# Score matmuls in bursts of three row-tiled pairs, with a hand-made order for the rest

The kernel runs on one core of a Trainium2 chip. The metric is the device time of one execution in microseconds (us). A run is called fast when it lies within 1.5% of the fastest of its kernel.

## The reference, cut to what matters

For each of 8 batches, with S = 3200 positions, D = 256 and a score width of 64:

```python
scores = (1.0 / S) * (z @ z.T)                 # z: S x 64, so S x S scores
x = u * (np.maximum(scores, 0.0) ** 2 @ v)     # u, v: S x 256
wq, wk = x @ w_q, x @ w_k                      # S x 64
mixed = (1.0 / 8.0) * (wq @ wk.T) @ x          # linear, so it can be x @ J with a 256 x 256 J
out = np.maximum(mixed, 0.0) @ w_out
```

Both kernels use `mixed = x @ (w_q w_k' (x'x)) / 8`. They need the sum x'x over all rows (X'X below), then a small matrix J, then two products per group of rows: `mx` (with J, then relu) and `fo` (with w_out). The large work is the scores and the product with v: 25 x 25 tiles of 128 x 128 per batch. In these kernels the operands of TensorE lie in a memory called SBUF, and its results in one called PSUM, which the kernels divide into banks. "Gate" below is relu and scaling of a score tile in PSUM, followed by a square into fp16 in SBUF.

## The kernel before

Score tiles are made in pairs. The 64 columns of z lie in SBUF twice, on partitions 0-63 and again on 64-127. One matmul of a pair uses the upper half of the array's rows and the other the lower half ("row tiling"), so that the two can run at once. A pair's out matmuls (with v) follow three pairs later. Which instruction comes when is left to the framework's scheduler, with priorities.

```python
psc = ... bufs=4, PSUM    # score tiles, one bank each
pacc = ... bufs=1, PSUM   # accumulator of a group of 512 or 384 columns, two banks
ptp = ... bufs=2, PSUM    # transposes, X'X, mx, fo
...
for pair in tpairs:                                  # two tiles, the last one alone
    for ti in pair:
        sc_ps = psc.tile([P, SG], FP32, tag="sc", name="sc_ps")
        half = (ti % 2) * dqk
        nc.tensor.matmul(out=sc_ps[:, 0:gw],
                         lhsT=zT2[half : half + dqk, ts(ti, P)],
                         rhs=zT2[half : half + dqk, ds(gs, gw)], start=True, stop=True)
    ...                                              # gate on VectorE (16 of 20) or ScalarE,
    ...                                              # square on ScalarE or GpSimd
    pending.append((ats, gi, out_ps, u_sb))
    if len(pending) > DEPTH:                         # DEPTH = 3
        emit_outs(*pending.pop(0))
# emit_outs: for each tile, gw // 128 matmuls of 256 columns into out_ps;
# at a group's end x = out_ps * u on VectorE, then transposes of x on TensorE
...
# emit_XJ(b), after a batch: 50 matmuls for X'X, then copy, product, copy, product, copy -> J
# emit_MX_chunk(b, jt, gi): mx and fo of the batch before, at the start of each group
```

Of the kernel before, what the change touches and what calls it, by code (L numbers as in the profile page):

```python
# [12 lines left out]
SQUARE = mybir.ActivationFunctionType.Square  # L13
# [4 lines left out]
def kernel(  # L18
# [10 lines left out]
    nc = tc.nc  # L29
# [6 lines left out]
    SG = 512  # L36
    sgroups = []
    s0 = 0
    for w in [512, 512, 512, 512, 384, 384, 384]:
        sgroups.append((s0, w))  # L40
        s0 += w
    assert s0 == S
    ND = D // P
    XPRI = 4 << 20
    SUPRI = 3 << 20
    HIPRI = 2 << 20
    MIPRI = 1 << 20
    DEPTH = 3
    tpairs = []
    ti = 0  # L50
    while ti < NT:
        tpairs.append(tuple(range(ti, min(ti + 2, NT))))
        ti += 2

    GSCALE = 4.0
    C1 = GSCALE * GSCALE
    ALPHA = C1 * float(S) * float(S)
    FINAL_SCALE = 1.0 / (8.0 * ALPHA * ALPHA * ALPHA)

# [5 lines left out]
    pg = ctx.enter_context(tc.tile_pool(name="pg", bufs=10))  # L65
    pat = ctx.enter_context(tc.tile_pool(name="pat", bufs=12))
    pjt = ctx.enter_context(tc.tile_pool(name="pjt", bufs=2))
    prt = ctx.enter_context(tc.tile_pool(name="prt", bufs=3))
    pfo = ctx.enter_context(tc.tile_pool(name="pfo", bufs=4))
    pmisc = ctx.enter_context(tc.tile_pool(name="pmisc", bufs=2))  # L70
    psc = ctx.enter_context(tc.tile_pool(name="psc", bufs=4, space=bass.MemoryType.PSUM))
    pacc = ctx.enter_context(tc.tile_pool(name="pacc", bufs=1, space=bass.MemoryType.PSUM))
    ptp = ctx.enter_context(tc.tile_pool(name="ptp", bufs=2, space=bass.MemoryType.PSUM))

    def emit_consts():
      ident32 = consts.tile([P, P], FP32, tag="ident32")
      make_identity(nc, ident32)
      ident = consts.tile([P, P], FP16, tag="ident")
      make_identity(nc, ident)

      wqk32 = consts.tile([P, 2, 2 * dh], FP32, tag="wqk32")
      nc.sync.dma_start(out=wqk32[:, :, 0:dh], in_=moe_w_q.rearrange("(c p) h -> p c h", p=P))
      nc.sync.dma_start(out=wqk32[:, :, dh : 2 * dh], in_=moe_w_k.rearrange("(c p) h -> p c h", p=P))
      wqT = consts.tile([P, D], FP32, tag="wqT")
      for ac in range(ND):
        wq_tp = ptp.tile([P, P], FP32, tag="tp", name="wq_tp")
        nc.tensor.transpose(wq_tp[0:dh, :], wqk32[:, ac, 0:dh], ident32)
        nc.scalar.copy(out=wqT[0:dh, ts(ac, P)], in_=wq_tp[0:dh, :])

      wo32 = consts.tile([P, 2, D], FP32, tag="wo32")  # L90
      nc.sync.dma_start(out=wo32[:], in_=moe_w_out.rearrange("(c p) e -> p c e", p=P))
      wo = consts.tile([P, 2, D], FP16, tag="wo")
      nc.vector.tensor_copy(out=wo[:], in_=wo32[:])
      return ident32, ident, wqk32, wqT, wo

    st = {}
    ld = {}

    def emit_load(b):
        z32 = pmisc.tile([P, NT, dqk], FP32, tag="z32")  # L100
        nc.sync.dma_start(out=z32[:], in_=z[b].rearrange("(n p) k -> p n k", p=P))
        zs = pmisc.tile([P, NT, dqk], FP16, tag="zs")
        nc.vector.tensor_copy(out=zs[:], in_=z32[:])
        zst = pmisc.tile([P, NT, dqk], FP16, tag="zst")
        nc.vector.transpose(out=zst[:, :, :], in_=zs[:, :, :])  # L105
        zT2 = pzt.tile([P, S], FP16, tag="zT2")
        for bk in range(dqk // 32):
            for bp in range(4):
                nc.sync.dma_start(
                    out=zT2[ds(32 * bk, 32), :].rearrange("j (n bp i) -> j n bp i", bp=4, i=32)[  # L110
                        :, :, bp, :
                    ],
                    in_=zst[ds(32 * bp, 32), :, ds(32 * bk, 32)],
                )
        nc.sync.dma_start(out=zT2[dqk : 2 * dqk, :], in_=zT2[0:dqk, :])
        v_sb = pv.tile([P, NT, D], FP16, tag="v_sb")
        nc.gpsimd.dma_start(out=v_sb[:], in_=v[b].rearrange("(n p) d -> p n d", p=P))
        ld[b] = (zT2, v_sb)

    def emit_A(b, mx_prev=None):  # L120
        zT2, v_sb = ld[b]
        x_sb = px.tile([P, NT, D], FP16, tag="x_sb")
        xT_sb = px.tile([P, ND, S], FP16, tag="xT_sb")
        st[b] = (x_sb, xT_sb)

        u_re = u[b].rearrange("(n p) d -> p n d", p=P)
        nat = 0

        def emit_outs(ats, gi, out_ps, u_sb):
            gs, gw = sgroups[gi]  # L130
            ngb = gw // P
            for ti, at in ats:
                for j in range(ngb):
                    nc.tensor.matmul(  # L134
                        out=out_ps[:, j // 2, ds((j % 2) * D, D)],
                        lhsT=at[:, ts(j, P)],
                        rhs=v_sb[:, ti, :],
                        start=(ti == 0 and j % 2 == 0),
                        stop=(ti == NT - 1 and (j % 2 == 1 or j == ngb - 1)),
                    )  # L140
            if ats[-1][0] == NT - 1:
                xtp = ptp.tile([P, ND, ngb, P], FP16, tag="tp", name="xtp")
                for j in range(ngb):
                    sb = gs // P + j
                    with tc.high_priority(offset=XPRI):
                        nc.vector.tensor_mul(  # L146
                            out=x_sb[:, sb, :],
                            in0=out_ps[:, j // 2, ds((j % 2) * D, D)],
                            in1=u_sb[:, j, :],
                        )  # L150
                    for db in range(ND):
                        nc.tensor.transpose(  # L152
                            xtp[:, db, j, :], x_sb[:, sb, ds(db * P, P)], ident
                        )
                for db in range(ND):
                    with tc.high_priority(offset=HIPRI):
                        nc.scalar.copy(out=xT_sb[:, db, ds(gs, gw)], in_=xtp[:, db])  # L157

        pending = []
        for gi, (gs, gw) in enumerate(sgroups):  # L160
            if mx_prev is not None:
                emit_MX_chunk(*mx_prev, gi)
            ngb = gw // P
            nbank = (ngb + 1) // 2
            out_ps = pacc.tile([P, nbank, 2 * D], FP32, tag="acc", name="out_ps")
            u_sb = pu.tile([P, ngb, D], FP32, tag="u_sb")
            nc.sync.dma_start(out=u_sb[:], in_=u_re[:, gs // P : gs // P + ngb, :])
            for pair in tpairs:
                ats = []
                for ti in pair:  # L170
                    sc_ps = psc.tile([P, SG], FP32, tag="sc", name="sc_ps")
                    half = (ti % 2) * dqk
                    nc.tensor.matmul(  # L173
                        out=sc_ps[:, 0:gw],
                        lhsT=zT2[half : half + dqk, ts(ti, P)],
                        rhs=zT2[half : half + dqk, ds(gs, gw)],
                        start=True,
                        stop=True,
                    )
                    ats.append((ti, sc_ps))  # L180
                for k, (ti, sc_ps) in enumerate(ats):
                    at = pat.tile([P, SG], FP16, tag="at")
                    g32 = pg.tile([P, SG], FP32, tag="g32")
                    m = nat % 20
                    with tc.high_priority(offset=SUPRI):
                        if m < 4:
                            nc.scalar.activation(
                                out=g32[:, 0:gw], in_=sc_ps[:, 0:gw], func=RELU, scale=GSCALE
                            )
                        else:  # L190
                            nc.vector.tensor_scalar(  # L191
                                out=g32[:, 0:gw], in0=sc_ps[:, 0:gw], scalar1=0.0,
                                scalar2=GSCALE, op0=AOP.max, op1=AOP.mult,
                            )
                    eng_act = (k + (nat // 2)) % 2 == 0
                    with tc.high_priority(offset=HIPRI):
                        if eng_act:
                            nc.scalar.square(out=at[:, 0:gw], in_=g32[:, 0:gw])  # L198
                        else:
                            nc.gpsimd.tensor_mul(  # L200
                                out=at[:, 0:gw], in0=g32[:, 0:gw], in1=g32[:, 0:gw]
                            )
                    nat += 1
                    ats[k] = (ti, at, eng_act)
# [137 lines left out]
```

## Time and profile before

The median was 1151.04 us (three runs, 1149.85 to 1153.22).

| | before |
|---|---|
| span of the profiled run | 1147.9 us |
| TensorE busy | 1067.0 us, 93% |
| next busiest, VectorE | 738.0 us, 64% |
| granted TensorE clock, mean | 0.989 |
| runs of score matmuls on TensorE (my count over the trace) | 701 |
| first score matmul | 31.8 us |

The head of the profile's page has, per engine, busy time, its share of the span, and the number of instructions. PE is TensorE, PEld its weight loads, DVE VectorE, ACT ScalarE and POOL GpSimd.

```profile
span 1147.9 us, 21719 instructions
PE 1067.0 (93%) x7890; PEld 637.7 (56%) x7890; DVE 738.0 (64%) x1329; ACT 679.2 (59%) x1355; POOL 665.7 (58%) x712
```

TensorE is the only engine near its limit, but 93% busy does not say that it streams without pause: an out matmul is booked as busy for 276 ns on average, while in a stream the next one starts after 109 ns. The timeline of TensorE in the middle of a 512-column group shows the pattern. Columns: start, length of the merged row (both us), engine, line, operation, tiles and count.

```profile
500.45 0.39 PE L173 MATMUL sc_ps<-zT_4064 64*128 64x512 f16 x2
500.77 1.05 PE L134 MATMUL out_ps<-v_sb,at 128*128 128x256 f16 x8
501.75 0.39 PE L173 MATMUL sc_ps<-zT_4064 64*128 64x512 f16 x2
502.07 1.05 PE L134 MATMUL out_ps<-v_sb,at 128*128 128x256 f16 x8
```

A period is 1.30 us: two score matmuls and eight out matmuls. The single records of the trace show where it goes (start in us, step from the start before in ns):

```
501.433  109   out matmul
501.543  110   out matmul, last of eight
501.748  205   score matmul, rows 0-63
501.751    3   score matmul, rows 64-127
502.070  319   out matmul, first of the next eight
502.189  119   out matmul
```

The two score matmuls do run together, 3 ns apart. But the step into them is 205 ns where out matmuls are 109 ns apart, and the step out is 319 ns where 512 columns in a stream without a change of tiling take 216 ns (seen in mx). Each trip into row tiling and back loses about 0.2 us, once per pair. The list of waits (who waited for what: total us, times, longest) shows the way in as "issue" in front of the weight loads of the scores, line 173, and also shows transposes waiting for x, line 152. These are the three rows with the most time in PE and PEld:

```profile
PEld L173 <- issue: 172.1, 703, 5.6
PEld L134 <- issue: 94.5, 449, 1.1
PEld L152 <- DVE x_sb L146: 53.9, 120, 0.8
```

This list counts idle time of the weight loads, which can stand still while TensorE streams; the single records are the measure of a trip. And not all of the 172.1 us are trips.

The Trainium skill, "TensorEngine Tiling (Array Packing)", Key Properties, says that changing the tiling mode drains TensorE. This trace agrees in that both steps across a change are longer than the ordinary ones, and gives the price.

### The profile page before, as it was taken

To read this page: it belongs to the slowest core of one execution; us is meant where nothing else is said; L and a number is where in the kernel's file an instruction comes from. 1 tells how busy PE (TensorE), PEld (TensorE's weight loads), DVE (VectorE), ACT (ScalarE), POOL (GpSimd) and SP (SyncE) were. 2 spreads that over 40 slices of the span, in tenths; PEclk is the share of its full clock that TensorE was granted. 3 is DMA by queue.
4 is the path that set the end of the run, shared out by engine and by line. 5 is a ranking of instruction groups with operands and counts; after the bars stand their busy time and mean duration, and the time that the engine had idled before them with its cause. 6 is when DMAs were issued, how large, how long until landed. Compare 5 with 4: busy or idle time off the path is not lost. (4 is left out here: it accounts for less than half of the span.)

```text
span 1147.9 us, 21719 instructions
## 1 busy us (share of the span) xinstructions
PE 1067.0 (93%) x7890; PEld 637.7 (56%) x7890; DVE 738.0 (64%) x1329; ACT 679.2 (59%) x1355; POOL 665.7 (58%) x712
## 2 busy tenths in 40 slices
PE   0899989999899998999979999999999999999996
PEld 0356555565555655555545555656565555656563
DVE  1497747677467764676736777477756776567760
ACT  0456646666466664666637665666656667566655
POOL 1468645666456664665636666467655666556650
PEclk9999999999999998999989999999999999999999
DMA  9843172011711128120181212711163112111103
GB/s 179 176 90 72 33 107 73 33 61 49 121 56 51 43 65 123 38 65 29 65 124 38 65 43 57 129 59 33 61 95 98 49 46 65 38 56 47 42 16 114
DMA packets 159132, 80.43 MB, mean 70 GB/s; under 512 B 81457, under 2 KB 158513, under 8 KB 159025
## 3 DMA queue, kind: packets, MB, share of 16 engines
q1 hardware_dynamic: 133296, 65.95, 22.7%
q0 software_dynamic: 25728, 13.11, 8.6%
q8 instruction: 61, 1.00, 0.4%
q14 instruction: 47, 0.38, 0.1%
HBM read 59.38 MB, written 26.21 MB: 75 GB/s over the span
## 5 line engine op out<-in xcount | busy, mean ns | idle before, releaser
L134 PE MATMUL out_ps<-v_sb,at 128*128 128x256 f16 x5000 | 670.8, 276 | 1.4 <-ACT at L198 1.4
L134 PEld LDWEIGHTS <-at 128*128 128x128 f16 x5000 | 443.2, 98 | 167.5 <-issue 94.5
L157 ACT COPY xT_sb<-xtp 128x512 f16<-128x512 f16 (+1 forms) x112 | 55.0, 543 | 44.0 <-PE xtp L152 43.6
L146 DVE TENSOR_TENSOR x_sb<-out_ps,u_sb 128x256 f16<-128x256 f32 x200 | 70.9, 414 | 14.3 <-PE out_ps L134 14.3
L273 ACT ACTIVATE rt<-mx_ps 128x512 f16<-128x512 f32 (+1 forms) x112 | 58.9, 555 | 28.2 <-PE mx_ps L265 28.1
L280 PE MATMUL fo_ps<-wo,rt 128*128 128x256 f16 x400 | 66.1, 286 | 8.1 <-ACT rt L273 5.2
L173 PE MATMUL sc_ps<-zT_103 64*128 64x512 f16 (+1 forms) x175 | 40.8, 380 | 34.0 <-DMA zT_103<-zst 31.8
L289 ACT ACTIVATE fo_sb<-fo_ps 128x512 f32<-128x512 f32 x112 | 56.0, 551 | 19.9 <-PE fo_ps L280 16.8
L265 PE MATMUL mx_ps<-xT_sb,jt 128*128 128x512 f16 (+1 forms) x224 | 60.3, 357 | 2.4 <-ACT rt L273 1.7
L152 PEld LDWEIGHTS <-x_sb 128*128 128x128 f16 x400 | 26.3, 97 | 63.4 <-DVE x_sb L146 53.9
L280 PEld LDWEIGHTS <-rt 128*128 128x128 f16 x400 | 34.4, 101 | 40.1 <-ACT rt L273 31.4
L152 PE MATMUL xtp<-ident,x_sb 128*128 128x128 f16 x400 | 53.3, 223 | 2.8 <-DVE x_sb L146 0.5
L105 DVE STREAM_TRANSPOSE zst<-zs 128x1600 f16<-128x1600 f16 x8 | 14.7, 1840 | 50.1 <-DMA u_sb<-in_u_dram 14.0
L220 PE MATMUL xtx_ps<-x_sb 128*128 128x256 f16 x400 | 46.8, 273 | 0.0
L173 PE MATMUL sc_ps<-zT_6108 64*128 64x512 f16 (+1 forms) x175 | 36.9, 365 | 6.6 <-DVE g_8223 L191 5.6
L173 PE MATMUL sc_ps<-zT_121 64*128 64x512 f16 (+1 forms) x175 | 36.6, 363 | 5.1 <-DVE g_2091 L191 3.9
L173 PE MATMUL sc_ps<-zT_4064 64*128 64x512 f16 (+1 forms) x175 | 37.1, 367 | 4.6 <-DVE g_6179 L191 3.6
L173 PE MATMUL sc_ps<-zT_2020 64*128 64x512 f16 (+1 forms) x175 | 37.1, 367 | 4.5 <-DVE g_4135 L191 3.5
L220 PEld LDWEIGHTS <-x_sb 128*128 128x128 f16 x400 | 38.1, 98 | 4.0
L173 PEld LDWEIGHTS <-zT_103 64*128 64x128 f16 x175 | 9.5, 93 | 54.4 <-DMA zT_103<-zst 31.8
L173 PE MATMUL sc_ps<-zT_12240 64*128 64x512 f16 (+1 forms) x175 | 36.1, 362 | 1.0 <-DVE g_14615 L191 0.2
L173 PE MATMUL sc_ps<-zT_10196 64*128 64x512 f16 (+1 forms) x175 | 36.1, 362 | 1.0 <-DVE g_12882 L191 0.2
(2838 smaller groups left out, 2120.4 us busy)
## 6 DMA issues: line engine op xcount, KB each, us to landing
out_dram<-fo_sb SPq DMA_DIRECT2D x88, 256.0 KB, 2.2
u_sb<-in_u_dram SPq DMA_DIRECT2D x32, 512.0 KB, 3.9
v_sb<-in_v_dram POOLq DMA_DIRECT2D x8, 1600.0 KB, 16.4
u_sb<-in_u_dram SPq DMA_DIRECT2D x24, 384.0 KB, 3.2
out_dram<-fo_sb SPq DMA_DIRECT2D x24, 128.0 KB, 2.1
z_97<-in_z_dram SPq DMA_DIRECT2D x1, 800.0 KB, 5.5
z_115<-in_z_dram SPq DMA_DIRECT2D x1, 800.0 KB, 21.2
z_2014<-in_z_dram SPq DMA_DIRECT2D x1, 800.0 KB, 9.8
```

The source lines that it names most:

```text
L105: nc.vector.transpose(out=zst[:, :, :], in_=zs[:, :, :])
L134: nc.tensor.matmul(out=out_ps[:, j // 2, ds((j % 2) * D, D)], lhsT=at[:, ts(j, P)], rhs=v_sb[:, ti, :], start=(ti == 0 and j % 2 == 0), st ...
L146: nc.vector.tensor_mul(out=x_sb[:, sb, :], in0=out_ps[:, j // 2, ds((j % 2) * D, D)], in1=u_sb[:, j, :],)
L152: nc.tensor.transpose(xtp[:, db, j, :], x_sb[:, sb, ds(db * P, P)], ident)
L157: nc.scalar.copy(out=xT_sb[:, db, ds(gs, gw)], in_=xtp[:, db])
L173: nc.tensor.matmul(out=sc_ps[:, 0:gw], lhsT=zT2[half : half + dqk, ts(ti, P)], rhs=zT2[half : half + dqk, ds(gs, gw)], start=True, stop=True,)
L220: nc.tensor.matmul(out=xtx_ps[:, cc, :], lhsT=x_sb[:, ti, ds(cc * P, P)], rhs=x_sb[:, ti, :], start=(ti == 0 and cc == 0), stop=(ti == NT ...
L265: nc.tensor.matmul(out=mx_ps[:, 0:gw], lhsT=jt[:, ac, ds(db * P, P)], rhs=xT_sb[:, ac, ds(gs, gw)], start=(ac == 0), stop=(ac == ND - 1),)
L273: nc.scalar.activation(out=rt[:, db, 0:gw], in_=mx_ps[:, 0:gw], func=RELU)
L280: nc.tensor.matmul(out=fo_ps[:, j - jf, :], lhsT=rt[:, dc, ts(j, P)], rhs=wo[:, dc, :], start=(dc == 0 and j == jf), stop=(dc == ND - 1 an ...
L289: nc.scalar.mul(out=fo_sb[:, 0:nj, :], in_=fo_ps[:, 0:nj, :], mul=FINAL_SCALE)
```

## The change

The intent is to pay the trip less often. The scores of six tiles (three pairs, in six PSUM banks) are made in one burst; then come the out matmuls of the burst before, with one piece of the other work ("filler": transposes with X'X, or J, or one mx, or one fo) in their middle. The order is written by hand. Gates and squares become 1024 columns wide. Groups are six of 512 columns and one of 128, in which up to four tiles share one bank. J is made from a precomputed w_q w_k', without two of its copies. The start loads only batch 0. The conversion and transposes of the next batch's z are cut into five pieces, one per burst. The core of the diff, with cuts marked:

```diff
-    for w in [512, 512, 512, 512, 384, 384, 384]:
+    while s0 < S:
+        w = min(BANK, S - s0)            # six of 512, one of 128
...
+    PAIRS = 3
+    BURST = 2 * PAIRS
+    bursts = [list(range(i, min(i + BURST, len(units)))) for i in range(0, len(units), BURST)]
-    psc = ... bufs=4   pacc = ... bufs=1   ptp = ... bufs=2
+    psc = ... bufs=3, PSUM   # slots of two banks: a score pair, or a filler
+    pacc = ... bufs=2, PSUM  # one bank each
...
+    def scores(members):                 # a pair: row half h, bank h of a slot
+        ps = slot("sc_ps")
+        for h, i in enumerate(members):
+            r = ds(h * dqk, dqk)
+            for t, c in pieces:
+                nc.tensor.matmul(out=ps[:, h, ds(c, gw)], lhsT=zT2[r, ts(t, P)],
+                                 rhs=zT2[r, ds(gs, gw)], start=..., stop=...)
...
+    def outs(members, at_middle, ready):  # at_middle: the filler
+        for (b, g), part in segs:         # units of the old group, then of the new one
+            if ends:                      # the group ends in this burst
+                for k in range(nk):
+                    for i in part:
+                        out_mms(i, k)
+                        step(width(i) // P // nk)
+                    x_make(b, g, k)       # VectorE: x = acc * u, frees the bank
...
+        for n, members in enumerate(bursts):
+            for pr in pairs:
+                tiles.append(scores(pr))
+            for q, pr in enumerate(pairs):
+                g32 = gate(tiles[q], pr, "act" if q == 1 else "dve")
+                ...                       # squares: q 0 GpSimd, q 1 ScalarE, q 2 later
+            outs(prev, middle, lambda i: rank[i])
+            for a in late:                # squares of q 2, one GpSimd, one ScalarE
+                square(*a)
```

## The prediction, made without seeing the result

> **What bounds it now.** TensorE. The busy table has PE at 93% of the 1147.9 us span, every other engine at 64% or less; the granted clock is 0.99. But busy is not streaming. Single records in the timeline (500 to 506 us, 512-wide group) show a period of 1.30 us per pair of score tiles: eight out matmuls 109 ns apart, then two score matmuls (rows 0-63 and 64-127) that start 3 ns apart and run together. The step from the last out matmul to the scores is 205 ns, not 109, and from the scores to the next out matmul 320 ns where 512 columns need some 213. So each round trip between full and row-tiled matmuls costs about 0.2 us. The Trainium skill ("TensorEngine Tiling (Array Packing)", Key Properties) says that changing the tiling mode drains TensorE; this trace agrees, and the list of waits books it as "issue" before the score weight loads: 172 us in 703 waits (some of it would be ordinary spacing). I count 701 runs of score matmuls. The rest of the loss: the start (first matmul at 31.8 us, behind the z placement), transposes waiting for x (54 us in 120 waits), XJ's serial chain of four copies per batch, and the tail.
>
> **What the change does.** 210 bursts of three pairs replace 701 runs. Where two pairs already ran back to back (87.0 us) they are 226 ns apart. A burst should cost 205+226+226+310-109, about 0.86 us; three single pairs cost 3x0.42=1.25 us. Saved: 0.39x210, about 80 us. Transposes and X'X move into one filler per burst, J loses two of its copies, the start no longer loads batch 1.
>
> TensorE afterwards, from measured spacings: outs 5000x0.109=544; scores with switches 185; transposes 22; X'X 44; mx 43; fo 44; f32 products for J 16. Sum about 898 us.
>
> Added outside that:
> - start: first burst near 26 us (only v of batch 0 competes with the z placement);
> - tail: seven mx-ACT-fo-ACT links, each about 3.1 us, over what TensorE needs there: 15 us;
> - group ends: x is made on VectorE behind both gates of the burst (two of about 1.15 us), and the next group's accumulator waits for it; by how much of the old group lies in the burst 0 to 2.5 us, mean about 1, x56: 50 us;
> - fillers whose PSUM slot comes back late, SyncE held by z placement, other: 20 us.
>
> That is about 1010 us with the 3 us by which the time exceeds the profile's span.
>
> **Other engines.** From 512- and 384-wide durations: 1024-wide ops need about 1.15 us on VectorE and 0.95 us on ScalarE, a 512-wide square 1.0 us on GpSimd. Per burst (TensorE about 4.3 us): VectorE 2.3 plus x work, ScalarE 2.4 plus 0.95 for a filler, GpSimd 3.0. None is the bound; the margin on ScalarE is the smallest.
>
> **Predicted:** 1010 us, range 960 to 1065. Faster by over 2%: 0.95; within 2%: 0.03; slower: 0.02.
>
> **What would show it right.** About 210 runs of score matmuls; pairs in a burst 226 ns apart; out matmuls still 109 ns apart; "issue" before score loads about 50 us; first matmul near 26 us; PE waits of 0.5 to 2.5 us at group ends, released by the multiplication that makes x; tail after the last out matmul 25 to 30 us.
>
> **What would make it wrong.** Pairs inside a burst not overlapping (weights of the next pair waiting for a drain: 370 ns apart) would cost some 60 us. Six score banks plus a filler share three slots: if evictions come late, every burst waits (0.3 us each is 60 us). If group ends hide, it is nearer 960.

## More of the kernel before

At four of the seven batch changes a score matmul waited 3.5 to 5.6 us, 16.6 us in all, for a gate on VectorE, and VectorE in turn stood 11.8 to 14.0 us in front of a transpose of a later batch's z. The first of the four:

```profile
171.21 1.84 DVE L105 STREAM_TRANSPOSE zst<-zs 128x1600 f16<-128x1600 f16 x1 [12.29 <-DMA zT_2020<-zst]
172.98 0.65 DVE L191 TENSOR_SCALAR g_2091<-sc_ps 128x512 f32<-128x512 f32 x1
173.69 0.37 PE L173 MATMUL sc_ps<-zT_121 64*128 64x512 f16 x1 [3.93 <-DVE g_2091 L191]
```

## The result

The median after was 1019.52 us (four runs, 1017.16 to 1020.08), before 1152.13 us (four runs). The ratio is 0.885, with a 95% interval of 0.883 to 0.887. Ratios here are from fast runs alone, and so not quite the ratio of the medians that are quoted.

The head of the page after, same columns:

```profile
span 1018.2 us, 19437 instructions
PE 922.2 (91%) x7896; PEld 659.3 (65%) x7896; DVE 654.4 (64%) x723; ACT 662.1 (65%) x754; POOL 671.6 (66%) x675
```

TensorE issued the same number of matmuls, within six, and was busy 145 us less; no other engine is near its limit. Its timeline in the first group (line 297 is the scores, 358 the out matmuls):

```profile
31.30 0.82 PE L297 MATMUL sc_ps<-zT_110 64*128 64x512 f16 x6
32.06 2.79 PE L358 MATMUL acc<-v_sb,at 128*128 128x256 f16 x24
34.78 0.82 PE L297 MATMUL sc_ps<-zT_110 64*128 64x512 f16 x6
35.54 0.72 PE L358 MATMUL acc<-v_sb,at 128*128 128x256 f16 x5
```

The period for three pairs is 3.48 us, against 3 x 1.30 = 3.90 us before. In single records, later in the run:

```
504.674  109   out matmul, last before the burst
504.879  205   score matmul      504.883    4   score matmul
505.105  222   score matmul      505.108    3   score matmul
505.321  213   score matmul      505.324    3   score matmul
505.633  309   out matmul
```

The trip is as dear as before (205 in, 309 out), but there are 209 of them instead of 701, and inside the burst pairs follow at the pace of their columns, 226 and 216 ns from the first matmul of a pair to the first of the next. From the list of waits after (other rows left out):

```profile
PEld L358 <- issue: 148.4, 256, 2.3
PE acc L358 <- DVE x_sb L376: 58.7, 69, 2.1
PEld L297 <- issue: 57.0, 212, 10.8
PE sc_ps L297 <- DMA zT_110<-zst: 10.1, 1, 10.1
```

"Issue" in front of the score loads fell from 172.1 (16.6 of it the four waits for a gate) to 57.0 us (10.8 of it once, at the start). The row of the out loads, line 358, grew, but the weight loads also stand still while TensorE itself waits for x or streams a burst, so it is no loss of its own. In place of the trips stands a wait that was not there before: out matmuls of a new group wait for the multiplication that makes x, because it frees the accumulator's bank. The timeline of all engines around the first such wait shows the order that causes it:

```profile
42.25 1.23 DVE L323 TENSOR_SCALAR g_391<-sc_ps 128x1024 f32<-128x1024 f32 x1 [1.12 <-PE sc_ps L297]
42.83 0.27 PE L358 MATMUL acc<-v_sb,at 128*128 128x256 f16 x1
43.39 1.22 DVE L323 TENSOR_SCALAR g_400<-sc_ps 128x1024 f32<-128x1024 f32 x1
44.52 1.28 DVE L376 TENSOR_TENSOR x_sb<-acc,u_sb 128x512 f16<-128x512 f32 x2
45.25 0.38 PE L358 MATMUL acc<-v_sb,at 128*128 128x256 f16 x2 [2.15 <-DVE x_sb L376]
```

TensorE finished the old group near 43.1 us, VectorE made both gates of the burst first, and x began at 44.52 us.

### The profile page after: what moved, and what is told of

Read it like the earlier page. It is cut to its first block, busy times and chain, and to the rows that moved or that the text cites. A ratio compares the mean times of both kernels' runs of the same rounds, so it can differ in the third digit from the quotient of the medians.

```text
span 1018.2 us, 19437 instructions
## 1 busy us (share of the span) xinstructions
PE 922.2 (91%) x7896; PEld 659.3 (65%) x7896; DVE 654.4 (64%) x723; ACT 662.1 (65%) x754; POOL 671.6 (66%) x675
## 5 line engine op out<-in xcount | busy, mean ns | idle before, releaser
L358 PE MATMUL acc<-v_sb,at 128*128 128x256 f16 x5000 | 624.1, 274 | 60.8 <-DVE x_sb L376 58.7
L259 ACT ACTIVATE rt<-mx_ps 128x1024 f16<-128x1024 f32 (+1 forms) x56 | 52.1, 930 | 34.8 <-PE mx_ps L251 34.8
L376 DVE TENSOR_TENSOR x_sb<-acc,u_sb 128x512 f16<-128x512 f32 (+1 forms) x104 | 66.4, 662 | 6.6 <-PE acc L358 5.9
L217 DVE COPY xT_sb<-xx_ps 128x1024 f16<-128x1024 f16 (+1 forms) x56 | 35.5, 634 | 53.2 <-PE xx_ps L210 52.6
L277 ACT ACTIVATE fo_sb<-fo_ps 128x1024 f32<-128x1024 f32 (+1 forms) x56 | 52.1, 930 | 21.3 <-PE fo_ps L269 18.3
L210 PE MATMUL xx_ps<-x_sb 128*128 128x256 f16 x400 | 55.9, 283 | 0.0
L127 POOL DMA_DIRECT2D v_sb<-in_v_dram x40 | 36.4, 910 | 0.8 <-POOLq L513 0.8
L297 PE MATMUL sc_ps<-zT_110 64*128 64x512 f16 (+1 forms) x175 | 23.7, 372 | 13.8 <-DMA zT_110<-zst 10.1
L205 PE MATMUL xx_ps<-ident,x_sb 128*128 128x128 f16 x400 | 32.8, 225 | 0.5 <-DVE x_sb L376 0.5
L225 DVE TENSOR_TENSOR xtx<-xx_ps,xtx 128x512 f32<-128x512 f32 x48 | 32.7, 681 | 0.0
L297 PE MATMUL sc_ps<-zT_773 64*128 64x512 f16 (+1 forms) x175 | 21.7, 356 | 0.0
L297 PE MATMUL sc_ps<-zT_10136 64*128 64x512 f16 (+1 forms) x175 | 21.7, 356 | 0.0
L297 PE MATMUL sc_ps<-zT_3823 64*128 64x512 f16 (+1 forms) x175 | 21.7, 356 | 0.0
L297 PE MATMUL sc_ps<-zT_5390 64*128 64x512 f16 (+1 forms) x175 | 21.7, 356 | 0.0
```

What stands on the lines that cost most here:

```text
L127: nc.gpsimd.dma_start(out=st[b]["v"][:, ds(c * n, n), :], in_=v[b].rearrange("(n p) d -> p n d", p=P)[:, ds(c * n, n), :],)
L205: nc.tensor.transpose(tp[:, db, j, :], x_sb[:, gs // P + j, ds(db * P, P)], cst["ident"])
L210: nc.tensor.matmul(out=ps[:, 1, ds(cc * D, D)], lhsT=x_sb[:, gs // P + j, ds(cc * P, P)], rhs=x_sb[:, gs // P + j, :], start=(j == 0 and c ...
L217: nc.vector.tensor_copy(out=xT_sb[:, :, ds(gs, gw)].rearrange("p d (j s) -> p d j s", s=P), in_=tp[:, :, 0:n, :],)
L225: nc.vector.tensor_add(out=xtx[:], in0=acc, in1=xtx[:])
L259: nc.scalar.activation(out=rt[:, :, 0:gw], in_=ps[:, :, 0:gw], func=RELU)
```

## The experiments

All nine kernels gave a correct result. Medians are of four runs; the kernel before had medians of 1151.2 to 1151.6 us beside them, so they can be compared with 1019.5 us (after) within a microsecond or so.

| run | median us | ratio to before |
|---|---|---|
| after | 1019.52 | 0.885 |
| e1 single pairs | 1105.61 | 0.961 |
| e2 two pairs and one | 1057.63 | 0.919 |
| e3 after without row tiling | 1096.61 | 0.952 |
| e4 narrow gates | 1025.74 | 0.891 |
| e5 before without row tiling | 1122.16 | 0.974 |
| e6 fillers in one lump | 1115.67 | 0.970 |
| e7 x before the second gate | 984.73 | 0.855 |
| e8 filler at the group's end | 1003.59 | 0.872 |
| e9 combination | 962.81 | 0.837 |

**Theory:** the gain is the number of trips between full and row-tiled matmuls. **Rival A:** it is the hand-made order. **Rival B:** it is the wider, fewer evictions. **Rival C:** row tiling pays as such, in both kernels.

### e1 and e2: the same instructions, more trips

The gates and squares move with their pairs, so the order on VectorE, ScalarE and GpSimd changes too, and not on TensorE alone; the numbers of instructions are those of after.

```diff
-            for pr in pairs:
-                tiles.append(scores(pr))
-            ... gates of all three pairs ...
-                outs(prev, middle, lambda i: rank[i])
+            place(first)                 # scores and gates of the first pair (e2: two pairs)
+            outs(prev, middle, ..., [(1 / 3, place(1)), (2 / 3, place(2))])   # e2: [(1 / 2, place(2))]
```

> The kernel after, with its three score pairs of a burst spread over the burst: one pair, a third of the out matmuls, the next pair, and so on. Same instructions on all engines, only their order on TensorE differs; about 628 runs of score matmuls instead of 209. Theory (the round trip between full and row-tiled matmuls is what was saved): a lone pair costs 205+309-109 = 405 ns against 843 ns for three together, so +0.37 us for each of 209 bursts, +78 us: about 1097 us, less perhaps 20 us because the x multiplications now come before the last gate and the group-end waits shrink. Rival (the gain is from the hand-made order, wider evictions and fillers, not from the bursts): within 1% of 1020 us.

> As the single-pairs run, but two pairs together and the third after half of the out matmuls: about 419 runs of score matmuls. Theory: half the dose, +0.18 us for each of 209 bursts, +39 us, about 1058 us, less up to 15 us at group ends. Rival: within 1% of 1020 us.

Measured: 1105.61 us with 625 runs of score matmuls and 1057.63 us with 417, against 1019.52 us with 209. Thus 208 trips more cost 38 us and 416 more cost 86 us: 0.18 and 0.21 us each. In the single records, the steps from matmul to matmul at their usual spacing, without waits, add up to 42 us more in e2 and 84 us more in e1, which is 0.20 us a trip both times. e2 as a whole looks cheaper because its profile has two stretches at half the TensorE clock, where those of after and e1 have six (see e7). The timeline of e1 has the period of the kernel before again, 1.30 us a pair:

```profile
516.69 0.39 PE L298 MATMUL sc_ps<-zT 64*128 64x512 f16 x2
517.01 1.05 PE L359 MATMUL acc<-v_sb,at 128*128 128x256 f16 x8
517.99 0.39 PE L298 MATMUL sc_ps<-zT 64*128 64x512 f16 x2
518.31 1.05 PE L359 MATMUL acc<-v_sb,at 128*128 128x256 f16 x8
```

So 86 of the 132 us that the change gained hang on the bursts; rival A is left with 46 us at most. e1 came out 9 us above the expectation for two reasons that the trace shows. A lone pair costs 205 + 320 - 109 = 416 ns, not the 405 that I had put down with the burst's exit of 309 ns: three lone pairs (1248 ns) against a burst (850 ns) are then 398 ns, times 209 bursts 83 us. And the group-end waits did not shrink (56.7 us of idle time against 58.7):

```profile
PE acc L359 <- DVE x_sb L377: 56.7, 61, 2.0
```

### e3 and e5: no row tiling, in both kernels

All 128 rows are used, that is both copies of z; the score is doubled and the gate's scale halved, so the result is the same.

```diff
-            r = ds(h * dqk, dqk)         # e5: lhsT=zT2[half : half + dqk, ...] likewise
+            r = ds(0, 2 * dqk)           # e5: zT2[:, ...]
-                ... scale=GSCALE / scalar2=GSCALE
+                ... scale=GSCALE / 2 / scalar2=GSCALE / 2
```

> The kernel after without row tiling: each score matmul uses all 128 rows (both copies of z, so twice the score; the gate's scale is halved, the result is the same). No change of mode, but the score matmuls of a pair run one after the other, 216 ns each. Theory: no 205 and 309 ns steps any more, spacing 109 to 216 throughout; scores cost about 272 us instead of 184 us, so +88 us, about 1108 us. If row tiling inside a burst were not what makes scores cheap, the time would stay near 1020 us.

> The kernel before without row tiling (all 128 rows, twice the score, gate scale halved; same result). Theory: a lone row-tiled pair costs 205+320-109 = 416 ns at 512 columns against 432 ns without tiling, 364 against 324 ns at 384 columns, and a lone single tile 416 against 216 ns, so in the kernel before row tiling was worth nothing: about 1125 us, between 1105 and 1150. Rival (row tiling pays in the kernel before as well): 1230 us or more, because 700 pairs would each lose some 0.2 us of overlap.

| | row-tiled | all rows |
|---|---|---|
| order of before | 1151.6 | 1122.2 |
| order of after | 1019.5 | 1096.6 |

This is the clearest result. In the kernel before, taking the row tiling out made it 2.6% faster (ratio 0.974, interval 0.972 to 0.977). In the kernel after, taking it out cost 77 us, where 88 were expected: the steps into, inside and out of the score runs grew by 90 us, but the idle time at group ends fell from 58.7 to 50.9 us. A burst of six then takes 1.30 us from its first matmul to the first out matmul (e3):

```profile
503.32 1.46 PE L297 MATMUL sc_ps<-zT 128*128 128x512 f16 x6
504.62 1.47 PE L358 MATMUL acc<-v_sb,at 128*128 128x256 f16 x12
```

The timeline of e5 shows the kernel before without row tiling:

```profile
501.17 0.59 PE L173 MATMUL sc_ps<-zT 128*128 128x512 f16 x2
501.60 1.04 PE L134 MATMUL out_ps<-v_sb,at 128*128 128x256 f16 x8
502.47 0.59 PE L173 MATMUL sc_ps<-zT 128*128 128x512 f16 x2
```

The score matmuls now run one after the other, 216 ns each, but the steps into and out of them are ordinary. The period is 1.30 us, the same as with row tiling: the overlap of a lone pair (213 ns) and its trip (0.2 us) cancel. By the steps in the trace of before, a 384-column pair cost 205+3+265-109 = 364 ns with row tiling against 2 x 163 = 326 without, and a lone single tile some 416 against 216 ns. The trace of before has 108 lone tiles, 240 lone pairs of 384 columns and 290 of 512 columns, so 108 x 0.20 + 240 x 0.038 - 290 x 0.016 = 26 us is my estimate for these three, near the 29 us measured, though no run takes them apart. The Trainium skill gives "Up to 2×" for a dimension of 64 or less ("TensorEngine Tiling (Array Packing)", Theoretical Speedup); here a lone pair got nothing, and a burst of three took 850 ns where 6 x 216 = 1296 would stand. Rival C falls.

The right column also bounds rival A in another way: without row tiling in either, the new order is worth 26 us, start and batch changes included.

### e4: narrow gates

```diff
     def areas(members):
         ws = [width(i) for i in members]
-        if len(set(ws)) == 1:
-            return [(0, len(ws), ws[0])]
         return [(h, 1, w) for h, w in enumerate(ws)]
```

> The kernel after with every 1024-wide gate and square issued as two 512-wide ones (VectorE and ScalarE instructions rise by about 420 each). Rival theory (the gain comes from fewer and wider evictions): a visible loss, 20 us or more. Theory (TensorE bounds, the other engines have room): the gates take some 0.1 us longer per burst, so only the group-end waits grow, by up to 8 us: 1018 to 1030 us.

Measured 1025.74 us, 6 us more; the steps of TensorE around scores kept their sums. Rival B falls: the halved instruction counts of VectorE and ScalarE, though the most visible difference in the page's head, are worth about half a percent.

### e6: the fillers in one lump

```diff
         if not hit:
             at_middle()
+        if any(f[0] == 1 for f in fillers):    # the batch is complete
+            while fillers:
+                run_filler()
```

> The kernel after, but at the end of a batch all of its fillers (J and the fourteen mx and fo pieces) run one after the other instead of one per burst. Same instructions. Theory (one filler per burst hides ScalarE's links): each batch pays what the tail of the kernel after shows, 25.7 us from the last x to the last eviction against 13 us of TensorE work, so about 12 us more for each of 7 batches: 1090 to 1115 us. Rival (the placing of the fillers is worth nothing): within 1% of 1020 us.

Measured 1115.67 us, 96 us more than after. The list of waits of e6 names the largest part: fo waits for ScalarE's relu of mx, 56 times.

```profile
PE fo_ps L269 <- ACT rt L259: 66.5, 56, 1.2
PE acc L358 <- DVE x_sb L376: 64.8, 79, 2.1
```

In the kernel after the same wait stands at 8.3 us in 7 times, all in the tail, so this wait is 58 of the 96 us. The rest, in J's links, the group ends and slow-clock steps among others, was not taken apart. So one filler per burst is hardly a source of gain over the kernel before, where TensorE's idle time in front of fo was only 8.1 us in all, but bursts without it would have given back more than they won.

### e7 and e8: the wait at group ends

In these two the edits are cut to their sense:

```diff
+            early = any(i in prev[:3] for i in last_of.values())   # e7: group ends early in the burst
             for q, pr in enumerate(pairs):
-                gate and square of q
+                if not (early and q == 2): gate and square of q
 ...
                     x_make(b, g, k)
+                gate and square of q 2, if held back                # e7
+                if not hit and fillers: hit = True; at_middle()     # e8
```

> The kernel after, but in a burst that finishes a group with its first three units or fewer, VectorE makes x before the second gate. TensorE's order is unchanged. Theory (x waits behind the gate): the trace of after shows x starting 1.4, 1.0 and 0.5 us after TensorE began to wait in these bursts; moved up, about 22 us of the 62 us of group-end waits go: about 998 us. Rival (the wait is the multiplication itself and the signalling, not the queue): within 0.5% of 1020 us.

> The kernel after, but a burst that finishes a group before its middle puts its filler right there instead of at the middle. Theory: the filler's 0.9 us of TensorE work covers part of the wait for x in two of six positions of the group end, where one is on hand; about 16 us less: about 1004 us. If the wait is not for x: no change.

e8 came out at 1003.59 us, as expected in the sum but partly by luck: the idle time at the group ends fell by 12.8 us where 16 were expected of it, and the slow steps that the next paragraphs count fell too, from 9.4 to 3.7 us.

```profile
PE acc L358 <- DVE x_sb L376: 45.9, 67, 2.1
```

e7 gave 984.73 us, 35 us less than after, where 22 were expected; the order of TensorE's instructions is exactly that of after. Around the first group end of e7, x now follows the first gate:

```profile
42.67 1.23 DVE L323 TENSOR_SCALAR g<-sc_ps 128x1024 f32<-128x1024 f32 x1 [1.12 <-PE sc_ps L297]
43.81 1.28 DVE L376 TENSOR_TENSOR x_sb<-acc,u_sb 128x512 f16<-128x512 f32 x2
44.55 0.38 PE L358 MATMUL acc<-v_sb,at 128*128 128x256 f16 x2 [1.02 <-DVE x_sb L376]
45.01 1.22 DVE L323 TENSOR_SCALAR g<-sc_ps 128x1024 f32<-128x1024 f32 x1
```

Summed over the trace, the excess of the steps that wait for x over 109 ns fell from 70.0 us in after to 44.4 us in e7. That is 26 us. Another 8 us are slow steps elsewhere: matmuls with nothing to wait for, but more than 20 ns above their usual spacing, add up to 9.4 us in after and 1.4 us in e7. The windows view of after, at one of these stretches, shows the reason (columns: window, length, busy us and count for PE, PEld, DVE, ACT, POOL, then the granted clock, the DMA share and GB/s):

```profile
470.00:478.00 8.00, 6.49 (x56) 4.38 (x55) 6.45 (x7) 5.22 (x6) 5.79 (x7) 1.00 0.01 3
480.50:483.20 2.70, 2.70 (x14) 1.82 (x12) 1.29 (x2) 0.00 (x0) 0.00 (x0) 0.50 0.43 151
```

TensorE had waited 1.71 us for x until 478.20 us, and from 480 us its clock was halved for about 3 us. In after, the six such stretches between the start and the last batch all follow a group-end wait of 1.7 to 2.15 us (some waits of that length had no such sequel). In e7 I find none, and its four runs had a mean granted clock of 0.997 to 0.999 against 0.989 to 0.992 in after.

But the length of a wait does not decide it: after has 16 waits of 1.71 us or more and six halvings, e8 has seven (two of 2.15 us) and none. In the clock records of each profile the changes lie whole multiples of 3.413 us apart. Cut into such stretches, the one before each of the six halvings had TensorE idle for 52 to 69% of it; among the others of after the most is 55%. In e7, e8 and e9, none of which has a halving before its last batch ends, the idlest stretch has 43, 52 and 36%; in e1, 49% was enough. So what seems to count is whether idle time fills about half of one such stretch, and the group-end waits supply much of that idle time. This is argued from the traces, not isolated by a run.

### e9: a version to beat both

It has the edits of e7 and e8. The last batch runs its mx one ahead of its fo, with fo evicted by VectorE. z of the first batch is turned by TensorE transposes instead of by VectorE and small DMAs.

> A version meant to beat both: the kernel after with x before the second gate and the filler at the group end (the two earlier runs together), the last batch's mx pieces one ahead of its fo pieces with fo's eviction on VectorE, and z of the first batch turned by TensorE instead of by VectorE and small DMAs. Theory, from the trace of after: group ends 62 us down to about 25, tail 29 us down to about 21, first score burst from 20.5 to 24.3 us down to about 12: about 962 us, between 945 and 985.

Measured 962.81 us (962.69 to 964.80), ratio 0.837 to before. The sum was right, the parts less so. The first out matmul came at 16.77 us instead of 27.86. The excess at group ends fell to 31.8 us. The tail, from the last out matmul to the end, only fell from 29.3 to 25.9 us, because the evictions now wait for output buffers still being written out:

```profile
947.84 1.23 DVE L313 TENSOR_SCALAR fo_sb<-fo_ps 128x1024 f32<-128x1024 f32 x1 [1.96 <-DMA out_dram<-fo_sb]
950.45 1.22 DVE L313 TENSOR_SCALAR fo_sb<-fo_ps 128x1024 f32<-128x1024 f32 x1 [1.39 <-DMA out_dram<-fo_sb]
```

## Why the prediction was right

It said 1010 us, range 960 to 1065; the result was 1019.52. Point by point:

| step | predicted | measured |
|---|---|---|
| runs of score matmuls | 210 | 209 |
| pair to pair inside a burst | 226 ns | 226 and 216 ns |
| cost of a burst over the outs | 0.86 us | 0.85 us (205+4+222+3+213+3+309-109 = 850 ns) |
| gain from the bursts | 80 us | 86 us (e1) |
| out matmuls apart | 109 ns | 109 ns |
| "issue" before score loads | 50 us | 57.0 us |
| TensorE's own work | 898 us | 894 us |
| start | first burst near 26 us | first scores 20.5 and 24.3 us, first out 27.9 us |
| tail after the last out matmul | 25 to 30 us | 29.3 us |
| waits at group ends | 50 us, 0 to 2.5 each | 70.0 us (58.7 us as idle time), up to 2.15 each |

"TensorE's own work" measured is the sum of the usual spacings of all matmuls outside scores (690.4 us), the steps inside bursts (100.6 us) and those into and out of them (116.4 us), less 14 us that the first two of these waited for z.

The reason it held is that each term was a spacing read from the old trace times a count read from the diff, and the one figure that the old pattern rarely showed, how pairs follow each other without a change of tiling, could be found in a place where two pairs happened to be adjacent (87.0 us). The mechanism that e1, e2, e3 and e5 confirm is the one it named. Its "ScalarE has the smallest margin, none is the bound" also held, with ScalarE at 65%.

The term most off was the group ends, by 20 us: the wait was predicted with its right cause (x behind both gates of the burst, shown by e7), but the mean over the six positions was taken as about 1 us where 70.0 / 56 = 1.25 us was measured. The slow steps after long waits, 9.4 us, were not in the list by name; "other, 20 us" covered them. That the sum missed by less than 10 us is in part luck: the group ends were 20 us too small, "other" and TensorE's own work together some 15 us too large.

The prediction did not divide the 46 us between before and e1: it named the start, the transposes waiting for x, J's chain and the tail as further losses, and not the stops of VectorE at batch changes. The traces place most of them. In the start, the 33rd out matmul came at 48.24 us in before and at 34.95 us in e1, 13 us earlier (the first one only 6 us earlier: until 47.9 us before ran at half clock, with steps of 213 ns between out matmuls).

From the first out matmul of a batch to that of the next, batches 2 to 5 took 139.0 to 140.9 us in before and 130.2 to 132.9 us in e1, 34 us less together; these follow the four batch changes at which VectorE stood in front of a transpose of z and the clock was halved for 3.4 to 6.8 us. Batches 6 and 7, without such a stop, took 133.0 us each in before and 136.5 and 132.5 us in e1, so there the new order with single pairs won nothing, although e1 has 76 runs of score matmuls fewer than before in the whole. No run isolates the z transposes: that their placing is worth most of the 34 us is argued. What J's shorter chain, the transposes of x and the narrow 384-column groups add stays open.

## What to carry to other kernels

Row tiling pays per visit, not per matmul: before counting on overlap, measure the steps into and out of the tiled stretch, and put enough tiled work into one visit; with one pair per visit, here, no tiling at all was faster. When TensorE is reordered by hand, look at what else the engine that frees its accumulator has to do first: moving one multiplication ahead of one gate was worth 35 us, some 8 of them through the clock. And give each burst a piece of unrelated TensorE work to hide the other engines' links.

## What the Trainium skill lacked or had wrong

- "TensorEngine Tiling (Array Packing)", Key Properties, says that a change of tiling mode drains TensorE, but gives no cost. Here it was 205 ns in and 309 to 320 ns out, where the steps without a change are 109 and 216 ns: about 0.2 us per round trip at full clock (e1, e2).
- The same page's Theoretical Speedup and "When to Use Tiling" go by the size of the dimension alone. With one pair of 512 columns per visit the period was 1.30 us with and without row tiling, and the kernel before got 2.6% faster without it (e5); with three pairs per visit, 850 ns instead of 1296 ns.
- "TensorE: Matmul & The Clock Gate", in its closing table, says to avoid TensorE gaps above about 3 us. Here the clock was halved (0.50 granted) for 3.41 us at a time after single waits of 1.7 to 2.15 us, in six places of the kernel after; not every such wait had this sequel (none of seven in e8). What fitted better was the idle share of fixed stretches of 3.41 us: 52 to 69% before the six halvings, at most 43, 52 and 36% in e7, e8 and e9, which had none.
